# Two weight loads moved behind the DMA transposes, and an instruction order planned anew, in a fused attention and token-mixing kernel

## The chip, the cores and the metric

The kernel runs on one core of a Trainium2 chip. The metric is the device time of one execution in microseconds, as the median of several runs; less is better. Five engines work side by side: TensorE (PE), VectorE (DVE), ScalarE (ACT), GpSimd (POOL) and SyncE (SP), which here issues every DMA.

## The reference

For x of 2048 tokens by 640 features the kernel computes `x + attention(xn) * silu(mlp(xn))`, where xn is the layer norm of x:

```
xn  = layernorm(x)                               # over the 640 features
q, k, v = heads(xn @ wqkv)                       # 32 heads of 20 features
s   = concat(softmax(q k^T / sqrt(20)) v) @ wo
h   = layernorm(xn)
u   = gelu(h^T @ w1 + b1)                        # mixes the tokens: 2048 -> 1536
y   = (u @ w2 + b2)^T                            # 1536 -> 2048
out = x + s * silu(y)
```

All inputs and the output are bf16. The scores are 32 heads x 2048 x 2048 numbers, each of which needs an exponential.

## The kernel before, in words

**Tiling.** The heads are taken in 8 groups of 4 (`NG`, `GH`), the queries in 4 blocks of 512 (`NTB`), the keys in 16 chunks of 128. A *pass* is one head group with one query block, 32 passes in all. A *unit* is one head, one key chunk and 512 queries: one score matmul (`emit_st`, L1200) into one PSUM bank. A pass has 64 units. Most units go through ACT: `emit_exp` (L1229) takes two or three banks (128x1024 or 128x1536) in one exp. Up to 5 key chunks of a pass (`RC`) go through VectorE instead, as *D units*: `emit_op1` (L1240) turns the scores into the bits of an exponential, and `emit_top` (L1264) makes three shifted copies, which four products with scaled values (`vs_steps`, L749) average. Products with the values (`pv_mm`, L1280) gather a pass in one PSUM bank; at its end `ep_steps` transposes and divides (L1374 to L1395).

**Start.** Rows of x are loaded in blocks of 128 (`dma_x`, L471), then normalised on VectorE (`ln_steps`: L526 to L537, a power on POOL at L540, and the scaling at L544, which writes `regC`). xn must be transposed into `xnT_sb`. Blocks 0 to 3 (group 0) go over PE (`xT_steps`, L593, copied by L603 and L606). Blocks 4 to 15 (groups 1 to 3) are transposed by DMA, one DMA a block (`xTd_steps`, L581). The weight columns of the first head group are copied with padding into `wp_sb` (`wp_step`, L712), and `qk_steps` (L621) makes q and k of head group 0; a step marked "ev" (L1034 to L1038) goes to ACT or VectorE in the start, and to VectorE later. V comes from `v_steps` (L729, and L636 for the later heads). `r2_steps` (L555 to L564) forms the second layer norm.

**Query and key weights.** `wqk_sb` has the 640 query and 640 key columns. Columns 0 to 255 of each (`dma_w` with 256 columns, slots `wq` and `wk`) are enough for the first head group and for projection 0. The other 384 columns of each (slots `wkr` and `wqr`) are needed by projections 1 to 4 (`dqk_steps(i)` for i > 0 and `dlast_steps`), which make q and k of the other groups, store them in DRAM (L662, L687) and load them back by head (`qkload_steps`, L701).

**The MLP** (`mlp_steps`, `act_steps`, L636 to L837) is spread over the attention as jobs; it needs the halved biases `b1h_sb` and `b2h_sb`, made by job `bias` (L1430, L1432) from what job `bload` loads (L1425, L1427). The weights w1 come in pieces (`dma_w1`, L766), the first two as job `w1a` when the second layer norm is ready. Products with wo (`op_mms`, L920, L925) and the residual end the kernel (`tail_fin`, L1563 to L1570).

**What sets the order.** The instruction order is written at build time by a planner (`schedule`), which simulates the engines with fixed costs: it picks the engine that is free first and the candidate of least priority number that is ready. `Prog._add` keeps the costs and turns dependences into semaphore waits; each engine then runs its list in order, so an instruction that waits holds up all that stand behind it. Jobs (`add_job`, `add_bank_job`) become active when their tags are done and `at` passes are begun. DMA steps go to SP at once when their turn in a job comes. Every 16 units `tune` sets 14 options of the planner from one string of `PLAN`.

Of the kernel before, what the change touches and what calls it, by code (L numbers as in the profile page):

```python
# [10 lines left out]
P = 128  # L11
# [28 lines left out]
class Prog:  # L40
# [7 lines left out]
    def __init__(self, nc, n_lanes=8):  # L48
        self.nc = nc
        self.n_lanes = n_lanes  # L50
        self.cengs = list(self.COMPUTE) + [f"d{i}" for i in range(n_lanes)]
        self.cidx_of = {c: i for i, c in enumerate(self.cengs)}
        self.tasks = {e: [] for e in self.COMPUTE}
        self.ctasks = {c: [] for c in self.cengs}
        self.gcount = 0
        self.lane_rr = 0
        self.known = {e: [0] * len(self.cengs) for e in self.COMPUTE}
        self.T = {e: 0.0 for e in self.COMPUTE}
        self.busy = {e: 0.0 for e in self.COMPUTE}
        self.pipe = 0.0  # L60
        self.alog = []

    def ready(self, eng, reads=(), writes=()):
        r = 0.0
        lat = self.LAT[eng]
        for s in reads:
            t = s.w
            if t is None:
                return 1e15
            if not (t.ceng == "pe" and eng == "pe"):  # L70
                r = max(r, t.fin + (lat if t.ceng != eng else 0.0))
        for s in writes:
            t = s.w
            if t is not None and not (t.ceng == "pe" and eng == "pe"):
                r = max(r, t.fin + (lat if t.ceng != eng else 0.0))
            for t in s.readers.values():
                if not (t.ceng == "pe" and eng == "pe"):
                    r = max(r, t.fin + (lat if t.ceng != eng else 0.0))
        return r

    def _add(self, eng, ceng, fn, reads, writes, name, extra_req=(), cost=100.0, tail=None):
# [28 lines left out]
        for tt in req.values():  # L110
            start = max(start, tt.fin + (self.LAT[eng] if tt.ceng != eng else 0.0))
        kn = list(self.known[eng])
# [20 lines left out]
        if ceng not in self.COMPUTE:  # L133
            start = max(start, 700.0)
            if tail is not None:
                self.T[eng] = start + cost
                t.fin = start + tail
            else:
                self.T[eng] = start + 450.0
                self.pipe = max(self.pipe, start + 600.0) + cost  # L140
                t.fin = self.pipe + (1200.0 if self.pipe < 2500.0 else 2800.0 if cost > 800.0 else 1400.0)
        else:
            self.T[eng] = start + cost
            self.busy[eng] += cost
            t.fin = start + cost + (self.TAIL[eng] if tail is None else tail)
        return t

    def pe(self, fn, reads=(), writes=(), name="pe", cost=250.0, tail=None, w=None):
        t = self._add("pe", "pe", fn, reads, writes, name, cost=cost, tail=tail)
        self.alog.append((t.t0, cost * 1.0 if w is None else w))  # L150
        return t
# [99 lines left out]
class _Kern:  # L251
# [55 lines left out]
    PLAN = (  # L307
        "00010000000000", "00000000000000", "00100000001000", "00000000000000", "30020000000000", "30023200011000",
        "11022210111100", "00000000000010", "00022010000010", "00000000000000", "10000000101100", "22012000101100",
        "00000000000000", "20000110000010", "21220110100010", "11212110100010", "00000000000000", "10001010000000",  # L310
        "30001010000000", "00000200000000", "00002210100110", "00002000000010", "00012000000010", "01000000000100",
        "00003000010000", "22000000000000", "30001000010000", "00000020000110", "00000000110000", "01100000000000",
        "00000100010000", "00003200010000", "30000000100000", "10101300000100", "21000300000100", "00020400000000",
        "22022000000000", "00000300100100", "00000000000000", "00000000100000", "20004000000000", "00014010000000",
        "20114000000000", "02000110100000", "02000100100000", "02200400100000", "02200410101100", "00001000000000",
        "00004300000000", "10004300000000", "11004100000000", "11004100000000", "11004100001010", "12004100001010",
        "00000000000000", "00100010010100", "10200000000000", "10201000000010", "20221000000000", "21221000100100",
        "00004000000000", "00000000000000", "00000200010000", "00102000100000", "00000000000000", "00103020001000",
        "00000000000000", "31000000001000", "31220000000000", "00000210000000", "01120000000000", "00000000000000",
        "00010201100100", "00204000001000", "30004000001000", "00020000000010", "00020100000000", "00000000000000",  # L320
        "00020000010010", "01000320001000", "00200320001000", "00000000000000", "00102100000100", "00004000000100",
        "10020410010000", "12122110010010", "11100300100100", "30200000000000", "00000000000000", "00000010000000",
        "00003000100000", "10003000000000", "12002000000000", "00000000000000", "02002000001000", "02022000000000",
        "20001020000010", "00000000000000", "00000300011000", "01000200010100", "00020010001100", "00020010001110",
        "10000000000000", "10000000101000", "10000000101000", "00004000000000", "00004300000000", "02010000100010",
        "00003000010000", "10020100000000", "10020300010010", "10220300011110", "10004020000000", "00000000000000",
        "32100000010100", "22102300010000", "20100310010000", "20104311010000", "00000000000000", "00004200110000",
        "02004200110000", "00024300110000", "00000000000000", "01200000000100", "20110220000000", "22114211010110",
        "01000000001000", "01002000001000", "00000000000000",
    )  # L330
# [76 lines left out]
    def schedule(self):  # L407
# [48 lines left out]
        def pe_cost(mode, c):  # L456
            if pe_mode[0] != mode:
                pe_mode[0] = mode
                return c + 105.0
            return c  # L460
# [757 lines left out]
        def emit_exp():  # L1218
# [5 lines left out]
            for i in range(n):  # L1224
# [191 lines left out]
        for g in range(GH):  # L1416
# [5 lines left out]
        add_job("qk1pad", pads, tuple(f"qk0_{w}_{tb}" for w in (0, 1) for tb in range(NTB)) + ("qk0_1_0a",), 41.0)  # L1422
        add_job("r2", r2_steps(), sum((xtag(gb) for gb in range(4)), ()), 43.0)
        add_job("bload", [
            ("dma", small(lambda e: e.dma_start(bload_sb[:, 0:FC], B_b1.rearrange("(fc p) -> p fc", p=P))), [], [S_("bl1")],  # L1425
# [6 lines left out]
            ("dve", lambda e: e.tensor_scalar(b2h_sb[:, :], bload_sb[:, FC:FC + NB], 0.5, None, ALU.mult), [S_("bl2")],  # L1432
             [S_("b2h")], "b2h", 120.0), ("tag", "bias")], ("bload",), 43.0)

# [164 lines left out]
        def act_deadline(T):  # L1599
            t_ = max(pr.T["act"], T)  # L1600
            for us, banks, grp in pexp:
                t_ += len(us) * 512 * 0.8335 + 50.0
            return t_ - (105.0 + 216.0 + 170.0 + 60.0)
# [248 lines left out]
        def loads():  # L1852
            a, d = pr.T["act"], pr.T["dve"] + 601.0 * len(dop1)
            pe = pr.T["pe"] + 54.0 * len(avail)
            for us, banks, grp in pexp:
                a += len(us) * 512 * 0.8335 + 50.0
                pe += 54.0 * len(us)
# [95 lines left out]
```

## Time and profile before

| | before |
|---|---|
| median of 8 runs | 768.51 us (766.2 to 771.5) |
| profiled execution | 767.57 us, span 765.8 us |
| PE busy | 731.5 us (96%), 10140 matmuls |
| DVE busy | 721.8 us (94%), 1362 instructions |
| ACT busy | 733.5 us (96%), 697 instructions |
| POOL busy | 13.7 us (2%) |
| exps on ACT (L1229) | 659 instructions, 712.9 us |
| granted TensorE clock, mean | 0.998 |
| DMA | 42.52 MB, 56 GB/s over the span |

A busy time is the time in which at least one instruction of the engine runs; neighbours overlap a little, so mean times of one instruction add up to more. The profile also lists, for a group of instructions, the idle time of its engine just before them and who ended it. The chain of waits follows the work that ended last back to what released each step. A timeline lists instructions by start and length in us.

### The profile page before, as it was taken

To read this page: it belongs to the slowest core of one execution; us is meant where nothing else is said; L and a number is where in the kernel's file an instruction comes from. 1 tells how busy PE (TensorE), PEld (TensorE's weight loads), DVE (VectorE), ACT (ScalarE), POOL (GpSimd) and SP (SyncE) were. 2 spreads that over 40 slices of the span, in tenths; PEclk is the share of its full clock that TensorE was granted. 3 is DMA by queue.
4 is the path that set the end of the run, shared out by engine and by line. 5 is a ranking of instruction groups with operands and counts; after the bars stand their busy time and mean duration, and the time that the engine had idled before them with its cause. 6 is when DMAs were issued, how large, how long until landed. Compare 5 with 4: busy or idle time off the path is not lost.

```text
span 765.8 us, 22869 instructions
## 1 busy us (share of the span) xinstructions
PE 731.5 (96%) x10140; PEld 242.1 (32%) x10140; DVE 721.8 (94%) x1362; ACT 733.5 (96%) x697; POOL 13.7 (2%) x19
## 2 busy tenths in 40 slices
PE   8889999999999999999999999999999999999997
PEld 3322233223333233232333323233333323332222
DVE  7679999999999999999999999999999999999997
ACT  4789999999999999999999999999999999999993
POOL 4200000000000000000000000000000000000000
PEclk9999999999999999999999999999999999999999
DMA  9564111110133112130110402222225600410101
GB/s 281 80 88 117 20 37 32 24 26 20 32 70 67 21 19 75 20 86 13 20 38 11 108 15 53 46 52 60 53 55 85 141 12 6 150 47 12 47 12 69
DMA packets 117142, 42.52 MB, mean 56 GB/s; under 512 B 75300, under 2 KB 115876, under 8 KB 116996
## 3 DMA queue, kind: packets, MB, share of 16 engines
q1 hardware_dynamic: 117044, 41.07, 23.6%
q8 instruction: 79, 1.29, 0.8%
q14 instruction: 19, 0.16, 0.1%
HBM read 26.37 MB, written 10.22 MB: 48 GB/s over the span
## 4 chain that ended last, share of the span: by engine, by line
ACT 67%; PE 24%; DVE 4%; DMA 3%; SPq 1%; issue 0%; DVEq 0%; ACTq 0%
ACT pt_sb L1229 65%; PE ps_all L1200 8%; PE ps_all L1280 7%; PE ps_all L636 7%; DVE dt_sb L1240 2%; PE ps_all L920 2%; PE ps_all L621 1%; DMA xnT_sb<-regC 1%; ACT zt_sb L827 1%; ACT zt_sb L832 1%; DVE dt_sb L1264 1%; DMA bload_sb<-in_B_b_dram 1%; DMA wqk_sb<-in_A_wqkv_dram 1%; SPq L1417 0%; DVE v_sb L1035 0%
## 5 line engine op out<-in xcount | busy, mean ns | idle before, releaser
L1229 ACT ACTIVATE pt_sb<-ps_all 128x1024 bf16<-128x1024 f32 (+1 forms) x659 | 712.9, 1216 | 5.7 <-PE ps_all L1200 4.7
L1240 DVE TENSOR_SCALAR dt_sb<-ps_all 128x512 uint16<-128x512 f32 x496 | 332.6, 684 | 20.9 <-PE ps_all L1200 19.2
L1200 PE MATMUL ps_all<-qk_sb 32*128 32x512 bf16 x2048 | 291.1, 385 | 22.2 <-ACT pt_sb L1229 16.8
L1264 DVE TENSOR_SCALAR dt_sb<-dt_sb 128x2048 uint16<-128x2048 uint16 x372 | 247.7, 687 | 1.5
L1200 PEld LDWEIGHTS ps_all<-qk_sb 32*128 32x128 bf16 x2048 | 75.7, 91 | 282.8 <-ACT pt_sb L1229 190.6
L1280 PE MATMUL ps_all<-dt_sb,vs_sb 128*21 128x512 bf16 x1488 | 127.3, 384 | 0.3 <-DVE dt_sb L1264 0.2
L1280 PE MATMUL ps_all<-pt_sb,v_sb 128*21 128x512 bf16 x1552 | 123.8, 383 | 0.0
L636 PE MATMUL ps_all<-regB,regA 128*32 128x128 bf16 (+1 forms) x1536 | 67.2, 301 | 0.4 <-DVE zt_sb L806 0.3
L636 PE MATMUL ps_all<-regC,regA 128*32 128x512 bf16 (+1 forms) x1536 | 66.6, 301 | 0.0
L1280 PE MATMUL ps_all<-dt_sb,v_sb 128*21 128x512 bf16 x496 | 49.1, 386 | 1.5 <-DVE tr_sb L1374 1.4
L636 PE MATMUL ps_all<-xnT_sb,wqk_sb 128*32 128x512 bf16 x640 | 47.9, 382 | 0.1
L1280 PEld LDWEIGHTS ps_all<-dt_sb,vs_sb 128*21 128x21 bf16 x1488 | 32.2, 91 | 41.8 <-issue 22.1
L1280 PEld LDWEIGHTS ps_all<-pt_sb,v_sb 128*21 128x21 bf16 x1552 | 28.9, 91 | 47.8 <-issue 38.5
L636 PEld LDWEIGHTS ps_all<-regB,regA 128*32 128x32 bf16 x1536 | 28.4, 96 | 27.6 <-issue 11.3
L636 PEld LDWEIGHTS ps_all<-regC,regA 128*32 128x32 bf16 x1536 | 28.5, 96 | 26.2 <-issue 12.3
L920 PE MATMUL ps_all<-wv_sb,xnT_sb 128*128 128x512 bf16 (+3 forms) x160 | 29.2, 302 | 0.3 <-DVE regC L935 0.2
L1374 DVE STREAM_TRANSPOSE tr_sb<-ps_all 128x512 f32<-128x512 f32 x32 | 22.7, 710 | 1.3 <-PE ps_all L1280 1.2
L636 PE MATMUL ps_all<-wv_sb,xnT_sb 128*32 128x480 bf16 x320 | 22.3, 369 | 0.0
L636 PEld LDWEIGHTS ps_all<-xnT_sb,wqk_sb 128*32 128x32 bf16 x640 | 14.5, 95 | 19.0 <-issue 7.9
L1280 PEld LDWEIGHTS ps_all<-dt_sb,v_sb 128*21 128x21 bf16 x496 | 12.4, 90 | 24.5 <-issue 16.9
L1035 DVE CAST v_sb<-ps_all 128x480 bf16<-128x480 f32 (+1 forms) x23 | 13.8, 601 | 3.4 <-PE ps_all L729 3.1
L806 DVE TENSOR_SCALAR zt_sb<-ps_all,b2h_sb 128x512 bf16<-128x512 f32 (+1 forms) x32 | 16.8, 545 | 0.0
(72 smaller groups left out, 288.9 us busy)
## 6 DMA issues: line engine op xcount, KB each, us to landing
regA<-in_B_w_dram SPq DMA_DIRECT2D x6, 1024.0 KB
regA<-in_B_w_dram SPq DMA_DIRECT2D x8, 768.0 KB
qk_sb<-qk_scratch_dram SPq DMA_DIRECT2D x56, 80.0 KB
qk_scratch_dram<-qs_sb SPq DMA_DIRECT2D x32, 128.0 KB
regA<-in_A_x_dram SPq DMA_DIRECT2D x6, 640.0 KB
ok_scratch_dram<-on_sb SPq DMA_DIRECT2D x96, 20.0 KB
out_dram<-regC SPq DMA_DIRECT2D x3, 640.0 KB
wqk_sb<-in_A_wqkv_dram SPq DMA_DIRECT2D x2, 480.0 KB
```

Source lines behind the costliest of these rows:

```text
L621: steps.append(("pe", lambda e, dc=dc, lhsT=lhsT: e.matmul(ps(bk, n), lhsT, xnT_sb[:, dc, tb * 512 + c0:tb * 512 + c0 + n], start=(dc == 0 ...
L636: fns.append(lambda e, c=c, e_=e_: e.matmul(oc(c, e_), lhsT[:, c:e_], rhs, start=start, stop=stop, tile_position=(0, c)))
L806: steps.append(("dve", lambda e, z=z, i=i, jj=jj: e.tensor_scalar(z[:, c0:c0 + n], ps(bk, n, i * n), 0.5, bias[:, jj:jj + 1], ALU.mult, AL ...
L827: steps.append(("act", lambda e: e.activation(tt_, tt_, AF.Tanh, scale=1.5957691216), [stt], [stt], f"th{j}", ac(640)))
L920: steps.append(("pe", lambda e, c=c, k=k: e.matmul(ap, oT_sb[0:k, c, b * 128:(b + 1) * 128], wo_ap[0:k, c, c0:c0 + n], start=(c == 0), sto ...
L1035: return lambda e: e.tensor_copy(dst, src)
L1200: pr.pe(lambda e, outp=outp, lhsT=lhsT, rhs=rhs, g=g: e.matmul(outp, lhsT, rhs, start=True, stop=True, tile_position=(32 * g, 0)), reads=[ ...
L1229: tk = pr.act(lambda e: e.activation(outp, inp, AF.Exp, scale=math.log(2.0) / 128.0), reads=[bank_slot[b] for b in banks[:n]], writes=[S_( ...
L1240: tk = pr.dve(lambda e: e.tensor_scalar(w, src, WOFF, 0.0, ALU.add, ALU.max), reads=[bank_slot[bk]], writes=[S_(f"dt{d['tl'][0]}_{g}")], n ...
L1264: tk = pr.dve(lambda e: e.tensor_scalar(dst, src, dk, None, ALU.add), reads=[S_(f"dt{b0}_{g}") for g in range(4)], writes=[S_(f"dt{b}_{g}" ...
L1280: pr.pe(lambda e: e.matmul(outp, lhsT, rhs, start=(k == 0), stop=last, tile_position=(0, 32 * g)), reads=reads, writes=[bank_slot[AB]], na ...
L1374: steps.append(("dve", lambda e: e.transpose(tr_sb[:, :], ps(AB)), [bank_slot[AB]], [S_("tr")], f"epT{q}", 632.0))
```

## The change

1. The loads of the last 384 key and query columns (`wkr`, `wqr`) leave the opening list of DMAs and become a job, `wr`, which is issued when the transpose of block 15 has been issued. Projections 1 to 4 now require that job's tag.
2. In the opening list the load of x blocks 6 and 7 comes after the first `wq` and `wk` loads.
3. Job `bias` may begin only at pass 2.2.
4. The planner's costs change: 31 ns more when VectorE waits for PE, 53 instead of 50 ns for an exp beside its elements, 112 instead of 105 ns for PE's change to score matmuls, less what PE has idled; the DMA transposes now queue on the planner's one DMA pipe (`pipe`) with the loads; and loads of fewer than 300 columns count 1.6 times.
5. `PLAN` is another table of the same form, with 129 strings.

```
@@ Prog
+        self.pe_end = 0.0
+    def lat(self, eng, src):
+        return 0.0 if src == eng else self.LAT[eng] + (31.0 if eng == "dve" and src == "pe" else 0.0)
...
-                r = max(r, t.fin + (lat if t.ceng != eng else 0.0))
+                r = max(r, t.fin + self.lat(eng, t.ceng))
...
             if tail is not None:
                 self.T[eng] = start + cost
-                t.fin = start + tail
+                self.pipe = max(self.pipe, start) + cost
+                t.fin = self.pipe - cost + tail
...
+        self.pe_end = self.T["pe"]
@@ PLAN
-        "00010000000000", "00000000000000", "00100000001000", ...
+        "00000000000010", "00000000000000", "00003000000000", ...
@@ pe_cost
-                return c + 105.0
+                return c + max(0.0, (112.0 if mode == "st" else 105.0) - max(0.0, pr.T["pe"] - pr.pe_end))
@@ dma_w and the opening list
-            dma(lambda e: e.dma_start(dst, src), [], [slot], f"dma_w{c0}", 640 * 2 * n)
-
-        dma_x(0, 1)
-        dma_x(1, 1)
-        dma_x(2, 1)
-        dma_x(3, 1)
+            dma(lambda e: e.dma_start(dst, src), [], [slot], f"dma_w{c0}", 640 * 2 * n * (1.6 if n < 300 else 1.0))
+
+        for b in range(4):
+            dma_x(b, 1)
         dma_x(4, 2)
-        dma_x(6, 2)
         dma_w(0, 256, wqk_sb[:, :, 0, 0:256], S_("wq"))
         dma_w(640, 256, wqk_sb[:, :, 1, 0:256], S_("wk"))
+        dma_x(6, 2)
         dma_w(1280, 640, wv_sb[:, :, :], S_("wv"))
         dma_x(8, 4)
         dma_x(12, 4)
-        dma_w(896, 384, wqk_sb[:, :, 1, 256:640], S_("wkr"))
-        dma_w(256, 384, wqk_sb[:, :, 0, 256:640], S_("wqr"))
@@ emit_exp, act_deadline, loads
-                        name=f"exp{us[0]}", cost=n * 512 * 0.8335 + 50.0)
+                        name=f"exp{us[0]}", cost=n * 512 * 0.8335 + 53.0)
@@ jobs
         add_job("r2", r2_steps(), sum((xtag(gb) for gb in range(4)), ()), 43.0)
+        rw = []
+        for w in (1, 0):
+            src = A_wqkv[:, 640 * w + 256:640 * w + 640].rearrange("(kc p) f -> p kc f", p=P)
+            rw.append(("dma", lambda e, src=src, w=w: e.dma_start(wqk_sb[:, :, w, 256:640], src), [],
+                       [S_("wkr" if w else "wqr")], f"wr{w}", 491520))
+        rw.append(("tag", "wr"))
+        add_job("wr", rw, ("xTd15",), 30.0)
...
-             [S_("b2h")], "b2h", 120.0), ("tag", "bias")], ("bload",), 43.0)
+             [S_("b2h")], "b2h", 120.0), ("tag", "bias")], ("bload",), 43.0, at=2.2)
...
-                    rest.append((at, f"dqk{i}_{w}_{tb}", dqk_steps(i, w, tb), (), 40.0, at - self.QK_LEAD))
+                    rest.append((at, f"dqk{i}_{w}_{tb}", dqk_steps(i, w, tb), (("wr",) if i > 0 else ()), 40.0, at - self.QK_LEAD))
...
-                    rest.append((at, f"dqk4_{tb}", dlast_steps(tb), (), 40.0, at - self.QK_LEAD))
+                    rest.append((at, f"dqk4_{tb}", dlast_steps(tb), ("wr",), 40.0, at - self.QK_LEAD))
```

More of the change, by code (lines that the diff above doesn't have):

```diff
@@ L60, in __init__ @@
         self.pipe = 0.0
+        self.pe_end = 0.0
         self.alog = []
+    def lat(self, eng, src):
+        return 0.0 if src == eng else self.LAT[eng] + (31.0 if eng == "dve" and src == "pe" else 0.0)
     def ready(self, eng, reads=(), writes=()):
         r = 0.0
-        lat = self.LAT[eng]
         for s in reads:
@@ L74, in ready @@
             if t is not None and not (t.ceng == "pe" and eng == "pe"):
-                r = max(r, t.fin + (lat if t.ceng != eng else 0.0))
+                r = max(r, t.fin + self.lat(eng, t.ceng))
             for t in s.readers.values():
                 if not (t.ceng == "pe" and eng == "pe"):
-                    r = max(r, t.fin + (lat if t.ceng != eng else 0.0))
+                    r = max(r, t.fin + self.lat(eng, t.ceng))
         return r
@@ L110, in _add @@
         for tt in req.values():
-            start = max(start, tt.fin + (self.LAT[eng] if tt.ceng != eng else 0.0))
+            start = max(start, tt.fin + self.lat(eng, tt.ceng))
         kn = list(self.known[eng])
@@ L307 @@
     PLAN = (
[L308 to L327, printed above, removed]
@@ L328 @@
-        "02004200110000", "00024300110000", "00000000000000", "01200000000100", "20110220000000", "22114211010110",
-        "01000000001000", "01002000001000", "00000000000000",
+        "00000000000010", "00000000000000", "00003000000000", "02202000000000", "30000020000000", "01210300000000",
+        "00220000000000", "20220000000100", "10020100100100", "10020100100100", "30000000000000", "00000000000000",
+        "01000020100100", "00000000000000", "00000020110000", "00120320110000", "00000000000000", "20020000110000",
@@ new lines @@
+        "30220410100000", "31220410100000", "00001200000000", "00004200000000", "01100100000000", "00202320000000",
+        "00000000000000", "00002100000000", "10002000000000", "20000000000010", "20002400100000", "00000000000000",
+        "30012000001000", "00000000000000", "00100000001000", "02100220001000", "00104220000010", "01004000000000",
+        "00000000000000", "00004300000000", "02000300000000", "00000000000000", "00000100000010", "10001300100010",
+        "00000000000000", "10020200000000", "11002000010110", "02002000000000", "00004400001000", "00000000000000",
@@ new lines @@
+        "10000010100000", "10000010000010", "10000010100010", "10000010100010", "12020010100010", "21000200000000",
+        "11013200001010", "01013200001010", "10100000000010", "10004020000000", "00000300000100", "01002300000110",
+        "10002310000010", "10020310000010", "10021310000010", "20000000000010", "00020000000010", "00020000000110",
+        "20020020000110", "02100400000000", "00000000000000", "00000310001000", "00000200001000", "00103200001000",
+        "00000000000000", "00010100000000", "00000000000000", "00010310000000", "00000200010000", "21004210100010",
@@ new lines @@
+        "00000000000000", "01000420011000", "00000000000000", "00002300000010", "00022000100000", "21022010100000",
+        "01103300010000", "00000000000000", "31000000000000", "32001000000000", "32001000000000", "12004300001100",
+        "12002300101100", "00000000000000", "00100101010000", "00000000100010", "00000400010000", "02003100000000",
+        "00000000000000", "00020200010000", "00000000000000", "11101000010100", "10120310000110", "10100010000110",
+        "00000000000000", "10020200000000", "10000220001000", "10000210011000", "10020210110000", "00010210100000",
@@ L330 @@
+        "32010210100010", "02000000100000", "12000001100000", "11000200100000", "11000100100100", "00000000000000",
+        "00000000010000", "00000000000000", "01001100000100", "00001000000000", "00001000011000", "00020010000110",
+        "02020010001110", "01020010011110", "21020200010110", "30013010000000", "01000000000010", "00000000000000",
+        "02002200000010", "02002201000010", "00000000000000",
     )
@@ L1601, in act_deadline @@
             for us, banks, grp in pexp:
-                t_ += len(us) * 512 * 0.8335 + 50.0
+                t_ += len(us) * 512 * 0.8335 + 53.0
             return t_ - (105.0 + 216.0 + 170.0 + 60.0)
@@ L1855, in loads @@
             for us, banks, grp in pexp:
-                a += len(us) * 512 * 0.8335 + 50.0
+                a += len(us) * 512 * 0.8335 + 53.0
                 pe += 54.0 * len(us)
```

## The prediction

> **What bounds the kernel now.** I read the page first (busy time by engine, slices), then stretches of time, then what ScalarE waits for, then the timeline of the start.
>
> ```profile
> PE 731.5 (96%) x10140; PEld 242.1 (32%) x10140; DVE 721.8 (94%) x1362; ACT 733.5 (96%) x697; POOL 13.7 (2%) x19
> ...
> L1229 ACT ACTIVATE pt_sb<-ps_all 128x1024 bf16<-128x1024 f32 (+1 forms) x659 | 712.9, 1216 | 5.7 <-PE ps_all L1200 4.7
> ```
>
> Three engines look equally full. The stretches separate them:
>
> ```profile
> 200.00:300.00 100.00, 98.26 (x1583) 33.90 (x1586) 97.43 (x185) 99.87 (x95) 0.00 (x0) 1.00 0.23 51
> ...
> 600.00:700.00 100.00, 94.89 (x1253) 30.53 (x1242) 95.53 (x178) 99.90 (x95) 0.00 (x0) 1.00 0.22 63
> ...
> 55.00:56.00 1.00, 0.00 (x0) 0.00 (x0) 0.42 (x2) 0.61 (x1) 0.00 (x0) 0.90 1.11 327
> 56.00:57.00 1.00, 0.60 (x4) 0.11 (x4) 1.00 (x3) 0.00 (x0) 0.00 (x0) 0.50 1.16 330
> 57.00:58.00 1.00, 0.99 (x16) 0.42 (x16) 1.00 (x3) 0.91 (x1) 0.00 (x0) 0.50 1.20 292
> ```
>
> (Columns: window, its length, busy us of PE, weight loads, DVE, ACT, POOL with counts, granted clock, DMA share, GB/s.) From 60 to 753.7 us ACT is never idle for more than about 1 us in all, so that stretch is as long as ACT's own work. The kernel can win only in the start (to 60 us), in the tail (753.7 to 765.8) or by less ACT work. ACT's timeline of the start, idle time in brackets:
>
> ```profile
> 8.98 1.28 ACT L712 ACT_TABLE_LOAD   x1 [8.98 <-DMA wqk_sb<-in_A_wqkv_dram]
> ...
> 14.48 6.88 ACT L1229 ACTIVATE pt_sb<-ps_all 128x1024 bf16<-128x1024 f32 x6
> ...
> 25.70 0.60 ACT L1037 ACTIVATE qk_sb<-ps_all 128x512 bf16<-128x512 f32 x1 [4.34 <-PE ps_all L621]
> ...
> 35.47 1.45 ACT L1229 ACTIVATE pt_sb<-ps_all 128x1536 bf16<-128x1536 f32 x1 [1.14 <-PE ps_all L1200]
> ...
> 41.24 2.37 ACT L1229 ACTIVATE pt_sb<-ps_all 128x1536 bf16<-128x1536 f32 x2 [0.66 <-PE ps_all L1200]
> ...
> 57.09 1.45 ACT L1229 ACTIVATE pt_sb<-ps_all 128x1536 bf16<-128x1536 f32 x1 [1.49 <-PE ps_all L1200]
> ...
> 59.91 2.54 ACT L1229 ACTIVATE pt_sb<-ps_all 128x1024 bf16<-128x1024 f32 x2 [1.37 <-PE ps_all L1200]
> ```
>
> After the first exp (14.48) these holes are 4.34 + 1.14 + 0.66 + 1.49 + 1.37 = 9.0 us. What is behind them, from the chain of waits (start, length) and VectorE's timeline:
>
> ```profile
> 18.48 4.80 DMA xnT_sb<-regC
> ...
> 37.30 2.70 DMA xnT_sb<-regC
> ```
>
> ```profile
> 24.62 0.69 DVE L1035 CAST qk_sb<-ps_all 128x512 bf16<-128x512 f32 x1 [3.51 <-PE ps_all L621]
> 25.23 1.51 DVE L544 TENSOR_SCALAR regC<-regA,st_sb 128x640 bf16<-128x640 bf16 x4
> ...
> 54.49 0.17 DVE L1430 TENSOR_SCALAR b1h_sb<-bload_sb 128x12 f32<-128x12 bf16 x1 [1.68 <-DMA bload_sb<-in_B_b_dram]
> ...
> 55.58 0.17 DVE L1432 TENSOR_SCALAR b2h_sb<-bload_sb 128x16 f32<-128x16 bf16 x1 [0.92 <-DMA bload_sb<-in_B_b_dram]
> ```
>
> The first two (chain of waits) are DMA transposes, issue to landing: 4.80 us for block 7, behind the input loads, but 2.70 us for block 15 on a quiet queue. The next two: VectorE sat 3.51 us on the key eviction of row block group 1, and the normalisation of blocks 8 to 11, which needed nothing from it, stood behind. The last two: the bias scalings wait for their load in VectorE's order, so the score evictions behind them are late, PE stops, and the granted clock falls to 0.50.
>
> **The change, part by part** (the changed program's order of instructions is taken from the built kernel).
>
> *ACT's work.* Score units through ACT stay 1552 (423x2 + 235x3 + 1 before, 428x2 + 232x3 after); D units stay 496. One exp more costs about 0.05 us (ten exps with 25 units took 11.40 us, so about 0.43 a unit and 0.05 an instruction). A fifth query/key eviction replaces one of V: 0.49 against 0.32 us of ACT's time. Together +0.2 us, on the path.
>
> *First exp.* The x load of blocks 6 and 7 moves behind the first wq/wk loads. wk then lands after 1.64 MB instead of 1.97 MB, at 300 GB/s about 1.1 us earlier. But ACT now evicts the first transposes between its two copies of wp, so all five query products wait for the second copy (about 11.7), the fifteen products end near 14.0 as before (13.84), and eight V products stand ahead of the first scores, where four did: first exp near 15.3 instead of 14.48, **+0.8** at that point. VectorE's key eviction now stands one BN_STATS earlier and delays blocks 4 and 5 by 0.4 us; the SP queue, one transpose per 1.3 to 1.6 us, absorbs most of that.
>
> *Late weights (L476 to a job behind the last transpose).* Two loads of 0.98 MB leave the queue ahead of the transposes. The input loads end about 2.7 us sooner (0.98 MB at the 362 GB/s of 12 to 13 us). Block 7 should land at 18.4 + 2.7 = 21.1 instead of 23.28; at best 2.2 us, at worst nothing. The reason for "nothing" is in the trace: between 19.0 and 22 us the DMA engines moved only 26, 157 and 50 GB/s, two pauses after the loads' last bytes, and one like them sits at 34 to 36 us with no load in flight. The Trainium skill's page "DMA: Bandwidth & Descriptors" (Queues, rings and completion order) says descriptors are consumed in ring order on each engine: by that alone the transposes gain the loads' whole 2.7 us, by the trace's quiet case 2.1. I take half, 22.2, **-1.1**. The same page (Rules for kernel authors) says to issue a DMA early and wait late, which speaks against late weights: a first use that waits would cost. Here the first use is projection 1, held to 3 passes of about 23 us, some 75 us; the weights land near 42. Nothing. The weight issue and both first w1 loads are now on SP ahead of the okz store, the four pad copies, the bias load and the query/key stores. Before, w1 stood behind these at 49.99 and held the first store to 55.33; w1 near 38 to 43 is out of its way.
>
> *ACT's hole at 21.4.* ACT fills it with 0.8 us of later exps, and now does the key eviction too: landing at 22.2 gives the first exp of group 1 at 22.2 + 2.9 = 25.1 (before 23.3 + 2.9 = 26.2). So hole plus late start is 1.1 us less, 21.1 would give 2.2.
>
> *Groups 2 and 3.* No key eviction stands ahead of blocks 8 to 11 now: their normalisation can start when POOL's power is done, about 22.2 instead of 25.23, and that group lands near 29.4 instead of 32.4, before ACT has used up group 1 (about 32.7). The hole of 1.14 shrinks to PE's own pattern: two key products now run ahead of the last score pair, about 0.55 is left, **-0.6**. Blocks 12 to 15 follow 2 us earlier; group 3 lands near 37.5 against a need near 38. The hole of 0.66 goes, unless a pause of 1.3 us strikes again; I take 0.4 left, **-0.3**.
>
> *Bias scaling (at=2.2).* It moves behind 24 score evictions instead of 6, tens of us after its load. The hole of 1.49 goes, and with it 1.37, which I put down to the clock: PE did the work from 57 to 59 us at 0.50. The skill's page "TensorE: Matmul & The Clock Gate" (What's actually happening) puts the drop after an idle window of about 3.4 us; here a pause of about 2 us was enough, while 2.4 us at 21 to 23 cost nothing. By the page's length the second hole would need another cause and stay, gain 1.5; by the clock row the gain is **-2.9**, which I take. Late next is nothing that the order shows.
>
> *Order written anew (PLAN, latencies).* VectorE's and PE's work is the same but for seven idle-filling matmuls. PE goes over to scores or away from them 24 times more (1190 against 1166), each about 0.1 us, 2.4 us of PE time in 685 us where it idles 20. ACT waited 0.9 us there; bounds for the change are -0.9 (nothing left) and +8 (all of PE's slack spent badly). I take **+0.5**, near the row of before.
>
> *Tail.* After the last product that needs the staged head block, VectorE did its 12 operations in 757.76 to 763.5 = 5.7 us, with gaps because ten 512-wide and 128-wide matmuls stood before the last pair. Now two blocks finish back to back and the other two have four and five matmuls ahead: twelve operations without gaps are 4 x (0.61 + 0.21 + 0.41) = 4.9. **-0.7**, bounds 0 and -0.9.
>
> Sum: +0.2 - 1.1 - 0.6 - 0.3 - 2.9 + 0.5 - 0.7 = -4.9 (the first exp's +0.8 is taken up inside the first hole and counts only if that hole closes). The profiled execution took 767.57 (span 765.8); the median of the runs is 768.51, 0.94 above it. So 768.5 - 4.9 = **763.6**. About 0.3%, 2.3 us, is what a measurement of this kernel can tell from no change.
>
> **Rivals.**
> *Quiet transposes.* The pauses come only from the loads: block 7 lands at 21.1 and nothing strikes group 3. Another -1.5, and no new stall in the steady part (-0.5): 761.6.
> *The pauses stay.* They are the transposes' own (34 to 36 us speaks for it): the late weights bring nothing, group 3 has a hole of 1.2. +1.1 + 0.8: 765.5.
> *The new order starves ACT (slower).* PE is 97 to 98% busy in the middle; if the new order puts its work badly, scores come late. It takes one mechanism: score groups that miss ACT's cycle. A cycle of five units is about 2.24 us, some 300 of them. To lose the 4.9 us gained and 2.3 more, ACT must wait 25 ns in each, its share from 60 to 750 us falling below 98.8%. At 60 ns a cycle it is 18 us less the gain: 768.5 - 5.4 + 18 = 781. Against it: the longest matmul stretches between scores are alike in both orders (three of 2.13 us in each).
> *It doesn't do what it says.* The holes only move (to the power, SP's queue or the tail): 768.
>
> **Chances.** Main case 0.40 (762.2 to 764.8), quiet transposes 0.20, pauses stay 0.20, holes move 0.10, starved 0.10. Faster by over 0.3% (below 766.2): the first three, 0.80. Within 0.3%: 0.11. Slower: 0.09. The range leaves out some of the quiet case below and the starved and part of the moved case above: 760.5 to 767.5.
>
> **What would show it.** Right: no wait on the bias load in VectorE's order, clock 1.00 from 50 to 60 us, the L544 of blocks 8 to 11 near 22, ACT's holes after the first exp near 4 us, ACT at 99.8% from 60 us. Wrong: ACT below 99% in the middle; block 7's transpose at 4.8 us again; a new wait of VectorE on PE in the start; a query/key store late enough that an eviction into qs_sb waits.

## The result and the profile after

| | before | after |
|---|---|---|
| median | 769.70 us (766.1 to 774.3, 32 runs) | 761.93 us (760.0 to 764.5, 11 runs) |
| ratio after / before | | 0.9903, 95% interval 0.9885 to 0.9920 |
| profiled execution (span) | 767.57 us (765.8) | 762.00 us (760.1) |

The changed kernel is faster by about 1.0%: 7.5 us by the ratio, 7.8 between these medians. The forecast was 763.6 us, 4.9 less than the 768.5 of the eight runs that were known then. The two profiled executions differ by 5.6 us, their spans by 5.7. (Line numbers of after are one to eight above those of before in the parts shown: the exp is L1230, the scores L1201, the key and query products L622.)

The page of the changed kernel, busy time and the exp's group:

```profile
PE 730.3 (96%) x10147; PEld 240.9 (32%) x10147; DVE 720.5 (95%) x1362; ACT 732.9 (96%) x698; POOL 13.2 (2%) x19
...
L1230 ACT ACTIVATE pt_sb<-ps_all 128x1024 bf16<-128x1024 f32 (+1 forms) x660 | 712.4, 1225 | 3.1 <-PE ps_all L1201 2.0
```

The work is the same within 1.3 us on every engine. What went is idle time of ScalarE: just before an exp it is 3.1 us in all, where it was 5.7, and before the evictions of queries and keys 3.5 instead of 5.6. Its timeline, idle time in brackets, shows which of it:

```profile
14.47 6.88 ACT L1230 ACTIVATE pt_sb<-ps_all 128x1024 bf16<-128x1024 f32 x6 [0.60 <-PE ps_all L1201]
23.07 0.60 ACT L1035 ACTIVATE qk_sb<-ps_all 128x512 bf16<-128x512 f32 x1 [1.72 <-PE ps_all L622]
24.15 0.60 ACT L1038 ACTIVATE qk_sb<-ps_all 128x512 bf16<-128x512 f32 x1 [0.48 <-PE ps_all L622]
24.64 7.80 ACT L1230 ACTIVATE pt_sb<-ps_all 128x1024 bf16<-128x1024 f32 x7
32.77 0.60 ACT L1038 ACTIVATE qk_sb<-ps_all 128x512 bf16<-128x512 f32 x1 [0.33 <-PE ps_all L622]
33.26 5.97 ACT L1230 ACTIVATE pt_sb<-ps_all 128x1536 bf16<-128x1536 f32 x5
...
39.68 22.69 ACT L1230 ACTIVATE pt_sb<-ps_all 128x1024 bf16<-128x1024 f32 x20
...
645.03 3.71 ACT L1230 ACTIVATE pt_sb<-ps_all 128x1536 bf16<-128x1536 f32 x3 [1.04 <-PE ps_all L1201]
```

From 33 us on ACT runs through: the holes at 41 us, 57 us and 60 us are gone. The first exp starts where it did (14.47, before 14.48), the exps of row block group 1 start at 24.64 instead of 26.19, after the same six exps. A new hole of 1.04 us stands at 645 us. In stretches:

```profile
55.00:56.00 1.00, 1.00 (x10) 0.27 (x8) 1.00 (x2) 1.00 (x2) 0.00 (x0) 1.00 1.17 51
56.00:57.00 1.00, 0.93 (x20) 0.43 (x20) 1.00 (x3) 1.00 (x2) 0.00 (x0) 1.00 0.82 113
...
200.00:300.00 100.00, 96.67 (x1471) 31.67 (x1467) 98.43 (x187) 99.98 (x99) 0.00 (x0) 1.00 0.23 54
600.00:700.00 100.00, 96.26 (x1174) 30.00 (x1171) 97.15 (x179) 98.95 (x94) 0.00 (x0) 0.98 0.18 58
```

At 55 to 57 us TensorE works at full clock, where before it stood still until 56.4 and went on at 0.50. From 200 to 300 us ACT is as full as it was (99.98 against 99.87). From 600 to 700 us it lost a microsecond, with the mean clock at 0.98.

In the chain of waits the DMA transpose of block 7 is now this, and in VectorE's timeline the normalisation of blocks 8 to 11 no longer stands behind a key eviction:

```profile
17.64 4.10 DMA xnT_sb<-regC
```

```profile
21.32 1.52 DVE L545 TENSOR_SCALAR regC<-regA,st_sb 128x640 bf16<-128x640 bf16 x4 [0.94 <-POOL st_sb L541]
```

Block 7 lands at 17.64 + 4.10 = 21.74 us (before 23.28). The sum from trace to trace, each time after minus before: ACT's idle time ahead of the exps of group 1 2.20 instead of 4.34, -2.14 (ACT makes one eviction more there, so these exps start only 1.55 us sooner); the hole of 1.14 now 0.33, -0.81; the hole of 0.66 gone, -0.66; the two bias holes gone, -2.86; ACT's idle time from 60 us to the last exp 2.28 instead of 0.92, +1.36; ACT's busy time 732.93 instead of 733.46, -0.53; the tail, from the end of the last exp, 11.95 instead of 12.1, -0.15. That is -5.8, where the spans differ by 5.7.

### The profile page after: what moved, and what is told of

Its sections match the earlier page's. It is cut to its first block, busy times and chain, and to the rows that moved or that the text cites. A ratio compares the mean times of both kernels' runs of the same rounds, so it can differ in the third digit from the quotient of the medians.

```text
span 760.1 us, 22883 instructions
## 1 busy us (share of the span) xinstructions
PE 730.3 (96%) x10147; PEld 240.9 (32%) x10147; DVE 720.5 (95%) x1362; ACT 732.9 (96%) x698; POOL 13.2 (2%) x19
## 4 chain that ended last, share of the span: by engine, by line
ACT 71%; PE 24%; DVE 3%; DMA 1%; issue 0%; SPq 0%; DVEq 0%
ACT pt_sb L1230 69%; PE ps_all L1201 8%; PE ps_all L637 7%; PE ps_all L1281 7%; ACT zt_sb L833 1%; PE ps_all L622 1%; ACT zt_sb L828 1%; DVE dt_sb L1241 1%; PE ps_all L921 1%; DMA xnT_sb<-regC 1%; DMA regA<-in_A_x_dram 0%; PE ps_all L676 0%; DVE dt_sb L1265 0%; DVE regC L1571 0%; DVE bst_sb L527 0%; DVE regC L545 0%
## 5 line engine op out<-in xcount | busy, mean ns | idle before, releaser
L1230 ACT ACTIVATE pt_sb<-ps_all 128x1024 bf16<-128x1024 f32 (+1 forms) x660 | 712.4, 1225 | 3.1 <-PE ps_all L1201 2.0
L1201 PE MATMUL ps_all<-qk_sb 32*128 32x512 bf16 x2048 | 289.7, 385 | 22.0 <-ACT pt_sb L1230 17.0
L1201 PEld LDWEIGHTS ps_all<-qk_sb 32*128 32x128 bf16 x2048 | 74.0, 91 | 279.7 <-ACT pt_sb L1230 182.0
L1281 PE MATMUL ps_all<-dt_sb,vs_sb 128*21 128x512 bf16 x1488 | 125.5, 383 | 0.7 <-DVE dt_sb L1265 0.6
L637 PE MATMUL ps_all<-regC,regA 128*32 128x512 bf16 (+1 forms) x1536 | 68.3, 301 | 0.0
```

Source lines behind the costliest of these rows:

```text
L637: fns.append(lambda e, c=c, e_=e_: e.matmul(oc(c, e_), lhsT[:, c:e_], rhs, start=start, stop=stop, tile_position=(0, c)))
L1201: pr.pe(lambda e, outp=outp, lhsT=lhsT, rhs=rhs, g=g: e.matmul(outp, lhsT, rhs, start=True, stop=True, tile_position=(32 * g, 0)), reads=[ ...
L1230: tk = pr.act(lambda e: e.activation(outp, inp, AF.Exp, scale=math.log(2.0) / 128.0), reads=[bank_slot[b] for b in banks[:n]], writes=[S_( ...
L1281: pr.pe(lambda e: e.matmul(outp, lhsT, rhs, start=(k == 0), stop=last, tile_position=(0, 32 * g)), reads=reads, writes=[bank_slot[AB]], na ...
```

## The experiments

Each kernel takes the list of instructions that the planner wrote, moves a few of them, and issues the list again, so that the rest of every engine's order stays as it was. Ratios are to runs of the kernel before that were made beside each experiment; a difference in us is the ratio's, on 769.7 us.

### e1_bias: the bias scalings late, alone

```
 before, order on VectorE
-  b1h, b2h where the planner put them (L1430, L1432)
+  b1h, b2h just ahead of the first operation of the MLP that needs them
```

> The kernel before, every engine's list as it was, but the two bias scalings stand later on VectorE, just ahead of the first MLP eviction. Theory (the bias load's wait held VectorE, and the clock fell because PE stopped): both holes of ScalarE, 1.49 and 1.37 us near 57 and 60 us, go, clock 1.00 from 50 to 60 us, 2.9 us less than before. Rival (only the first hole is the wait's, the second has a cause of its own): 1.5 us less, a hole of about 1.4 us stays. Rival (hidden): no difference.

Measured: 766.68 us, ratio 0.9971 (0.9954 to 0.9989), 2.2 us less than before, between 0.8 and 3.5. ACT's timeline, at the first hole and from the third on:

```profile
27.09 0.60 ACT L1062 ACTIVATE qk_sb<-ps_all 128x512 bf16<-128x512 f32 x1 [5.37 <-PE ps_all L646]
...
42.96 2.36 ACT L1254 ACTIVATE pt_sb<-ps_all 128x1536 bf16<-128x1536 f32 x2 [0.45 <-PE ps_all L1225]
...
45.92 17.50 ACT L1254 ACTIVATE pt_sb<-ps_all 128x1536 bf16<-128x1536 f32 x15
```

Both late holes go together when VectorE no longer waits for the bias rows. The time alone does not choose between the 2.9 us of the forecast and the 1.5 that follow from the idle window of about 3.4 us in the Trainium skill's page "TensorE: Matmul & The Clock Gate" (What's actually happening). The trace does: both holes belong to this wait, and in before a pause of 2.07 us was long enough for the clock to fall.

This profiled execution is no shorter than that of before (span 765.7 against 765.8), for reasons outside the edit. Its first exp starts 0.36 us later, ACT loses 0.58 us behind a fall of the clock near 667 us, and, most of all, its first hole is 5.37 us instead of 4.34. The order there is that of before, but the clock fell after TensorE's wait for block 7's transpose, and the ten products behind it took 3.30 us instead of 2.33:

```profile
23.75 3.30 PE L646 MATMUL ps_all<-xnT_sb,wp_sb 128*128 128x512 bf16 x10 [2.44 <-DMA xnT_sb<-regC]
```

```profile
25.00:26.00 1.00, 1.00 (x5) 0.30 (x3) 0.96 (x2) 0.00 (x0) 0.00 (x0) 0.50 0.00 0
```

(The first line is from TensorE's timeline, the second is a stretch.) So the early weights cost clock at the start in some executions of the kernel before, though not in the one that was profiled as before.

### e2_weights: the late weights, alone

```
 before, order of DMAs on SP
-  dma_w (384 key columns), dma_w (384 query columns) ahead of the transposes
+  both just behind the transpose of block 15
```

> The kernel before, but the two loads of 384 columns stand behind the last DMA transpose on SP; nothing else is moved. Theory (the transposes queue behind the loads): block 7 lands 1.5 to 2.2 us sooner (near 21.5 instead of 23.3), the start moves up with it, 1.5 to 2 us less. Rival (the pauses are the transposes' own): it lands at 23 again, no difference. The hole at the bias wait stays in both.

Measured: 765.90 us, ratio 0.9957 (0.9938 to 0.9976), 3.3 us less, between 1.8 and 4.8. The chain of waits and ACT's timeline:

```profile
19.25 2.73 DMA xnT_sb<-regC
```

```profile
24.39 0.60 ACT L1062 ACTIVATE qk_sb<-ps_all 128x512 bf16<-128x512 f32 x1 [3.04 <-PE ps_all L646]
...
39.51 2.37 ACT L1254 ACTIVATE pt_sb<-ps_all 128x1536 bf16<-128x1536 f32 x2 [0.23 <-PE ps_all L1225]
...
54.28 1.45 ACT L1254 ACTIVATE pt_sb<-ps_all 128x1536 bf16<-128x1536 f32 x1 [0.40 <-PE ps_all L1225]
56.26 5.91 ACT L1254 ACTIVATE pt_sb<-ps_all 128x1024 bf16<-128x1024 f32 x5 [0.53 <-PE ps_all L1225]
```

Block 7 lands at 21.98, and the first hole falls from 4.34 to 3.04: 1.3 us. That is more than executions differ by: counted from the first exp, block 7 lands after 8.8 to 9.0 us in the five profiles with early weights (before, e1, e3, k1 and u1) and after 7.3 to 7.5 in the four with late weights that show it (e2, e4, t1 and the changed kernel). The rest is a gain that the forecast had not listed under this edit: the bias holes shrink from 1.49 and 1.37 to 0.40 and 0.53. The bias load lands earlier (VectorE's second scaling runs at 52.98 instead of 55.58), so TensorE waits 1.21 us there instead of 2.07, and the clock stays at 1.00. The bias wait is therefore shortened by two edits, and by the traces their gains overlap by up to 1.9 us. The times are too coarse to show it: e1 and e2 make 5.5 us together, all three moves at once (e4) 5.0.

### e3_norm: the normalisation of blocks 8 to 11 early, alone

```
 before, order on VectorE
-  key eviction of group 1 (L1035); scaling of blocks 8 to 11 (L544, x4)
+  scaling of blocks 8 to 11 (L544, x4); key eviction of group 1 (L1035)
```

> The kernel before, but VectorE's four scalings of blocks 8 to 11 stand ahead of the key eviction of group 1. Theory: they start near 22.2 instead of 25.2, group 2 of the transposes lands near 29.4 instead of 32.4, the hole of 1.14 us shrinks by at most 0.6 (the rest is PE's own order: key products, eviction, scores), the hole of 0.66 goes; about 1 us less. Rival (the hole of 1.14 is not the transposes'): it stays at 1.1, under 0.7 us less.

Measured: 769.59 us, ratio 1.0006 (0.9989 to 1.0023): nothing. VectorE's and ACT's timelines:

```profile
22.78 1.52 DVE L569 TENSOR_SCALAR regC<-regA,st_sb 128x640 bf16<-128x640 bf16 x4 [1.12 <-POOL st_sb L565]
...
35.99 1.45 ACT L1254 ACTIVATE pt_sb<-ps_all 128x1536 bf16<-128x1536 f32 x1 [1.15 <-PE ps_all L1225]
...
57.50 1.45 ACT L1254 ACTIVATE pt_sb<-ps_all 128x1536 bf16<-128x1536 f32 x1 [1.35 <-PE ps_all L1225]
59.49 2.54 ACT L1254 ACTIVATE pt_sb<-ps_all 128x1024 bf16<-128x1024 f32 x2 [0.54 <-PE ps_all L1225]
```

The scaling moved (22.78; before 25.23), and the hole stays at 1.15, so VectorE's order was not its cause. This run also shows something that it was not made for: the first bias hole is 1.35, the second 0.54 rather than 1.37. A stretch of this kernel, and TensorE's timeline:

```profile
56.00:57.00 1.00, 0.00 (x0) 0.00 (x0) 0.79 (x3) 0.15 (x1) 0.00 (x0) 1.00 1.15 344
```

```profile
57.03 0.40 PE L1225 MATMUL ps_all<-qk_sb 32*128 32x512 bf16 x4 [2.16 <-DVE dt_sb L1265]
```

TensorE stood still for 2.16 us here (2.07 in the profile of before) and kept its clock at 1.00. So of the 1.37 us, 0.83 was the clock at 0.50 in that one execution. The other 0.54 stands at full clock too. By TensorE's timeline it is the order of its work: 24 products stand between two groups of scores, so the second group starts 2.03 us after the first (59.06 and 57.03), while ACT's exp of the first takes 1.45.

### e4_all: the three moves together

```
 before
+ the moves of e1_bias, e2_weights and e3_norm
```

> The kernel before with the three moves together: bias scalings late, weights late, scalings of blocks 8 to 11 early; the rest of the order as before. If the moves explain the gain, 5 to 6 us less than before, within 2 us of the changed kernel (7.5 less), and the holes after the first exp add up to about 4 us. Rival (the gain is the new table's): under 4 us less.

Measured: 763.59 us, ratio 0.9935 (0.9911 to 0.9960), 5.0 us less. ACT's timeline:

```profile
24.05 0.60 ACT L1070 ACTIVATE qk_sb<-ps_all 128x512 bf16<-128x512 f32 x1 [2.78 <-PE ps_all L654]
...
34.01 1.45 ACT L1262 ACTIVATE pt_sb<-ps_all 128x1536 bf16<-128x1536 f32 x1 [1.15 <-PE ps_all L1233]
...
39.77 2.37 ACT L1262 ACTIVATE pt_sb<-ps_all 128x1536 bf16<-128x1536 f32 x2 [0.65 <-PE ps_all L1233]
...
42.73 19.76 ACT L1262 ACTIVATE pt_sb<-ps_all 128x1536 bf16<-128x1536 f32 x17
```

About two thirds of the change are these moves. The exps of group 1 start at 24.73, where the changed kernel's start (24.64), so the new order brings nothing until then. What it adds is that the holes of groups 2 and 3, 1.15 + 0.65 here, are 0.33 after: 1.5 us, as much as the two spans differ by (761.6 and 760.1). The ratios of the two kernels, 0.9935 and 0.9903, have intervals that overlap, so this part rests on the traces.

### u1_weights_early: the weights early again, in the changed kernel

```
 after, order of DMAs on SP
+  both loads of 384 columns (job wr) right behind the load of x blocks 12 to 15
-  both loads behind the transpose of block 15
```

> The changed kernel, with the loads of the key weights and of the late query weights back right behind the wp copies, ahead of the seven DMA transposes; everything else as in the changed kernel. Theory (the weights in flight hold up the transpose of block 7 and with it the first hole of ScalarE): block 7 lands at about 23 us rather than 21.74, the first hole grows from 1.72 to about 3.0 us, the time is 1 to 3 us above the changed kernel's 762. Rival (what counts is the new order of the start alone, the weights are free): within 0.5 us of 762.

(Twelve transposes follow these loads, not the seven of the expectation.) Measured: 765.09 us, ratio 0.9931 (0.9909 to 0.9954). That is above the changed kernel by 2.2 us if the ratios are compared, by 3.2 if the medians are; the two intervals just overlap. ACT's timeline, TensorE's, and a stretch:

```profile
25.66 0.60 ACT L1060 ACTIVATE qk_sb<-ps_all 128x512 bf16<-128x512 f32 x1 [4.54 <-PE ps_all L647]
```

```profile
23.30 3.74 PE L647 MATMUL ps_all<-xnT_sb,wp_sb 128*128 128x512 bf16 x10 [2.81 <-DMA xnT_sb<-regC]
```

```profile
23.00:24.00 1.00, 0.70 (x2) 0.28 (x3) 1.00 (x4) 0.00 (x0) 0.00 (x0) 0.50 0.64 124
```

Block 7 lands at 23.26, 1.5 us later than in the changed kernel, as expected. But the first hole grows by 2.8 us, and the exps of group 1 start 3.2 us later, counted from the first exp. The rest is the clock: TensorE waited 2.81 us for the transpose, its clock fell to 0.50, and the ten products took 3.74 us, against 2.33 in the changed kernel, where the wait is 1.05 us. So in this execution the early weights cost 1.5 us of landing and 1.4 us of clock. The clock's part does not come in every execution, and it is not the new order's alone. With early weights TensorE waits 2.35 to 2.81 us here, and the clock fell in two of five profiles (e1 and u1). With late weights it waits 0.82 to 1.08 us, and the clock fell in none of five.

### k1_clock: TensorE kept busy through the bias wait

```
 before, order on TensorE, ahead of the score pair that waits at 54 us
+  7 products 128x512 of zeros into a bank that is overwritten next
```

> The kernel before, with seven more 128x512 products of zero data into a bank of PSUM that the waiting scores do not use, queued on TensorE ahead of the score pair that waits while VectorE waits for the bias rows; their results are read by nobody. Theory (the second of the two late holes is TensorE recovering from a clock of 0.50 after its pause): the first bias hole of ScalarE stays near 1.5 us, the second goes from 1.37 to under 0.3 us, the granted clock stays at 1.00 from 50 to 60 us, and the time is 1.2 to 1.5 us below the kernel before. Rival (the second hole comes from the order of TensorE's work after the pause, or the filling itself delays the scores): both holes stay, and the time is that of the kernel before or up to 1 us above.

Measured: 768.56 us, ratio 0.9979 (0.9964 to 0.9994), 1.6 us less. ACT's timeline:

```profile
56.88 1.45 ACT L1257 ACTIVATE pt_sb<-ps_all 128x1536 bf16<-128x1536 f32 x1 [1.41 <-PE ps_all L1228]
58.86 3.57 ACT L1257 ACTIVATE pt_sb<-ps_all 128x1024 bf16<-128x1024 f32 x3 [0.54 <-PE ps_all L1228]
```

The clock was 1.00 throughout, the first hole stayed, and the second fell to 0.54, not under 0.3. Both theories missed: the clock was part of that hole, and 0.54 of it stays at full clock. The trace alone can't credit the zero products, for e3_norm has the same 0.54 and clock 1.00 without them. The lower median would fit if before falls to 0.50 there in some executions and this kernel does not; that was not shown run by run.

### x1_rows_late: no rows in flight during the transposes

```
 after, order of DMAs on SP
-  load of x blocks 12 to 15 ahead of the transposes
+  the same load behind the transpose of block 7
```

> The changed kernel, with the load of the rows of blocks 12 to 15 issued behind the DMA transpose of block 7 rather than ahead of it. Theory (a DMA transpose pauses while an ordinary load issued ahead of it is still in flight): block 7's transpose takes 2.7 to 3.2 us from issue to landing rather than 4.1, the first hole of ScalarE falls from 1.72 to 0.4 to 0.9 us, and the time is 0.8 to 1.4 us below the changed kernel's. Rival (the pauses are the transposes' own, or the late rows hold up the third query group): 4 us to landing as before, or a new hole near 30 us, and a time within 0.4 us or above.

Measured: 762.56 us, ratio 0.9918 (0.9891 to 0.9944), the changed kernel's time. TensorE's wait and the stretches of the pause:

```profile
21.45 2.33 PE L647 MATMUL ps_all<-xnT_sb,wp_sb 128*128 128x512 bf16 x10 [0.88 <-DMA xnT_sb<-regC]
```

```profile
17.00:18.00 1.00, 0.80 (x9) 0.19 (x6) 1.00 (x4) 1.00 (x2) 0.00 (x0) 1.00 1.51 83
18.00:19.00 1.00, 0.04 (x5) 0.02 (x3) 1.00 (x3) 1.00 (x2) 0.00 (x0) 1.00 1.47 48
```

The key products start 7.14 us after the first exp, 7.31 in the changed kernel: the landing hardly moves. A pause from 17 to 19 us, in which the DMA engines count as busy but move only 83 and 48 GB/s, is there without this load. The theory fell: the last load of rows isn't what the transposes pause for.

### t1_tail: the last value products first, block 14 first

```
 after, order on TensorE behind the last exp's scores
-  12 products of wo, last 4 value products, 19 products of wo, ...
+  10 products of wo, last 4 value products, the rest; blocks 14, 15, 12, 13
 order on VectorE
-  three operations a block, interleaved over two blocks
+  three operations a block, block after block
```

> The changed kernel, with the last four probability-times-value products of TensorE put ahead of the twelve output products in front of them, and block 14's output products and VectorE operations ahead of those of blocks 12 and 13. Theory (the tail gained only 0.15 us because the last value products stood behind output products): the last exponential to the end takes about 10.9 us rather than 11.95, and the time is about 1 us below the changed kernel's. Rival (VectorE's twelve operations or the last store set the end whatever stands ahead): 11.5 to 12 us, and a time within 0.4 us.

Measured: 761.52 us, ratio 0.9894 (0.9872 to 0.9916), 0.4 us below the changed kernel's median, which is within the noise. The tail takes 11.48 instead of 11.95 us. TensorE's and VectorE's timelines of the tail in this kernel:

```profile
748.48 0.40 PE L1327 MATMUL ps_all<-pt_sb,v_sb 128*21 128x512 bf16 x4
...
751.38 0.45 PE L972 MATMUL ps_all<-wqk_sb,stage_sb 128*128 128x128 bf16 x2
```

```profile
751.87 0.69 DVE L1617 TENSOR_TENSOR regC<-ps_all,regC 128x512 bf16<-128x512 f32 x1 [0.66 <-PE ps_all L972]
...
757.16 0.49 DVE L1621 TENSOR_TENSOR regC<-regC,regA 128x640 bf16<-128x640 bf16 x1
```

VectorE begins its last twelve operations 3.5 us after the last exp's end instead of 4.7, as the theory wants, but then takes 751.87 to 757.65 = 5.78 us for them, where the changed kernel took 4.88, so 0.9 was given back. Whether VectorE's new order or TensorE's gave it back is open: the early products with VectorE's interleaved order were not run.

## Why the prediction was right, point by point

**ACT's work, +0.2.** It went down by 0.5; the one exp more is there (660 for 659), but its 712.4 us are 0.5 fewer.

**First exp, +0.8, absorbed.** Wrong: 14.47. The step that failed is "all five query products wait for the second copy". The second copy began at 11.27, when the query products had already started. The fifteen products ran from 10.88 to 13.33 without a stop, while the second copy ended at 11.80; before, they had stopped 0.37 us for ACT's copy of the transposes.

**Late weights, -1.1, "I take half, 22.2".** Right in kind, too small: block 7 lands at 21.74, 1.54 us sooner, short of the 2.1 of the quiet case, and the exps of group 1 start 1.55 earlier. Alone the move is worth 3.3 us (e2), and undoing it costs 2.2 to 3.2 (u1). Two terms were missing: the bias load behind these weights lands earlier as well (e2), and a TensorE that waits less kept its clock in every profile. "Nothing" for the late first use holds: the trace shows no wait on these weights.

**Group 2, -0.6.** The size came (-0.81), the first reason was wrong: moving the normalisation alone does nothing (e3). The second reason given, two key products ahead of the last score pair, fits the traces. TensorE's timelines, before and after:

```profile
32.44 2.12 PE L621 MATMUL ps_all<-xnT_sb,wp_sb 128*128 128x512 bf16 x9
34.48 0.61 PE L1280 MATMUL ps_all<-pt_sb,v_sb 128*21 128x512 bf16 x8
```

```profile
30.83 1.90 PE L622 MATMUL ps_all<-xnT_sb,wp_sb 128*128 128x512 bf16 x8
```

Before, nine key and query products (2.04 us from start to start) and eight value products (0.55 us) stood between two groups of scores; after, eight products (1.83 us) and no value products. That order was not tested by itself, so the right size is in part luck.

**Group 3, -0.3.** 0.66 went altogether. This hole is TensorE's wait for the last DMA transposes, as its timeline of before shows:

```profile
40.05 0.82 PE L621 MATMUL ps_all<-xnT_sb,wp_sb 128*128 128x512 bf16 x3 [0.96 <-DMA xnT_sb<-regC]
```

In every profile with the old order the hole is this wait less 0.3 us: 0.96 and 0.66 here, 0.74 and 0.45 in e1, 0.54 and 0.24 in k1, 0.53 and 0.23 in e2, 0.94 and 0.65 in e4. It differs as much between executions with early weights as with late ones, so the late weights alone do not close it. In the changed kernel the scaling of blocks 12 to 15 runs at 29.60 (31.94 before, 30.38 in e4), and TensorE does not wait. Which part of the new order did that is open.

**Bias, -2.9.** Both holes are gone. But the working, a second hole of 1.37 that is all clock, was over one third wrong: 0.83 was clock, and 0.54 stays at full clock. Since the whole wait went, the sum stood.

**New order, +0.5.** ACT's idle time in the middle went up by 1.36, 1.04 of it at one place, behind the fall of the clock at 641 us. That fall is not shown to be the new order's: e1 and e3, with the old order, have one near 667 us, behind which ACT is idle for 0.6 and 0.7 us. The slower rival is excluded: ACT is busy for 99.98% of 200 to 300 us and 99.7% of 60 to 740.

**Tail, -0.7.** Mis-sized: 0.15 came. The step "twelve operations without gaps" held (4.88 for 5.72), but they began later. TensorE's and VectorE's timelines of the changed kernel:

```profile
747.23 1.58 PE L921 MATMUL ps_all<-wv_sb,xnT_sb 128*128 128x128 bf16 x12
748.74 0.40 PE L1281 MATMUL ps_all<-pt_sb,v_sb 128*21 128x512 bf16 x4
749.07 3.51 PE L921 MATMUL ps_all<-wv_sb,xnT_sb 128*128 128x512 bf16 x19
752.42 0.71 PE L926 MATMUL ps_all<-wqk_sb,stage_sb 128*128 128x128 bf16 x4
```

```profile
752.89 0.69 DVE L1571 TENSOR_TENSOR regC<-ps_all,regC 128x512 bf16<-128x512 f32 x1 [1.42 <-PE ps_all L926]
```

The last exp ends at 748.15, the last value products start 0.59 us later behind twelve others, and the products of the staged block, ready at 751.47, wait 0.95 us behind nineteen.

**The sum.** The forecast was 4.9 us less. The profiled executions came to 5.6 less, the ratio to 7.5. The 4.9 is right in its main terms, the bias wait and the late weights, and in part by luck: single terms missed by 0.5 to 0.9 us in both directions (ACT's work, the late weights and the two groups brought more, the order and the tail less), and these misses nearly cancel. What lies between 5.6 and 7.5 is outside one execution. Over the runs of each kernel the time falls as the mean clock rises: by 0.55 us per 0.001 in 29 runs of before (correlation -0.89; -0.76 in 20 others) and by 0.40 in 12 of after (-0.91). At a mean clock of 1.00 these lines give 766.3 and 760.7. Before's median clock was 0.995, after's 0.997; the profile of before happened to be one at 0.998. By this some 2 us of the 7.5 are clock that before loses in its usual executions and not in the profiled one. The profile of e1, with its fall in the start, shows one such loss. For the rest this is a correlation, not an experiment.

## What to carry to other kernels

Price a moved load by every wait behind it on the queue and by the clock of the engine that waits, not only by the transfer that it makes room for: the move was worth 3.3 us where its first landing gained 1.3. The gains of two edits that shorten the same wait can't simply be added. When a wait is put down to an instruction in front, look also at what the releasing engine does between its two releases; by the traces that explains one hole of 1.1 us here, though it was not tested alone. And look at the same place in several profiles before a hole is explained: the first hole was 4.3 to 5.4 us in four executions with the same order at that place.

## What the runs showed of the hardware

The granted clock can fall while TensorE counts as busy. Stretches of the changed kernel:

```profile
640.00:641.00 1.00, 0.75 (x11) 0.21 (x11) 1.00 (x4) 1.00 (x2) 0.00 (x0) 1.00 0.00 0
641.00:642.00 1.00, 1.00 (x11) 0.12 (x8) 1.00 (x3) 1.00 (x2) 0.00 (x0) 0.61 0.00 0
642.00:643.00 1.00, 1.00 (x10) 0.23 (x10) 1.00 (x3) 1.00 (x2) 0.00 (x0) 0.50 0.00 0
```

No pause above 0.31 us stands in the six microseconds ahead of it, but only 5 to 16 matmuls a microsecond ran there, where 18 to 20 ran earlier (628 to 633 us). A low count alone is not the cause: from 650 to 740 us the same kernel runs 9 to 11 a microsecond at 1.00. u1_weights_early and t1_tail fall near the same place, x1_rows_late not there but at 707 us, and e1_bias and e3_norm, with the old order, near 667 us. A cause was not tested.

These runs show no fixed length of a pause at which the clock falls. At the bias wait, with the same order of TensorE around it, 2.07 us brought 0.50 (before) and 2.16 us did not (e3_norm). At block 7's wait, with the same order again, 2.44 us did (e1_bias, and only about 1.2 us after TensorE had gone on) and 2.38 and 2.52 us did not (before, k1_clock).
